# Attention: the token-row transfers of three batches placed behind later scaled x

## The chip, the cores and the metric

The kernel runs on one core of a Trainium2 chip. The metric is the device time of one execution in microseconds (us). The engines have these names in the profile: PE (TensorE, matrix products; PEld are its weight loads), DVE (VectorE), ACT (ScalarE), POOL (GpSimd) and SP (SyncE, which here issues DMAs). Each engine works through its own queue in order and waits there for semaphores that other engines or DMAs set.

## The reference, cut to what matters

Three stages follow each other: causal attention with a decay for 4 batches of 8 heads, 576 tokens and 64 channels, a mixture of 8 experts of which each token takes one, and a gated block.

```python
def _attn_ref(q, k, v, f):
    scores = scale * np.matmul(q, k.transpose(0, 1, 3, 2))
    cum = np.cumsum(np.log(np.clip(f, 0.0001, 1.0)), axis=-1)
    scores = np.where(causal, -1e9, scores + cum[:, :, :, None] - cum[:, :, None, :])
    attn = softmax(scores)                       # max, exp, sum + 1e-9
    return np.matmul(attn, v)

def _moe_ref(x, w_gate, w_output_gate, w1, w2):  # x: 2304 tokens x 512
    logits = x @ w_gate
    e_idx = np.argmax(logits, axis=1)
    ...
    for e in range(E):
        mask = e_idx == e
        ye = np.maximum(x[mask] @ w1[e], 0.0) @ w2[e]
        out[mask] = gate_w[mask, None] * eom[mask, e, None] * ye

def _moe2_ref(x, w_gate, w_val, w_out):
    return ((1 / (1 + np.exp(-(x @ w_gate)))) * (x @ w_val)) @ w_out
```

## The kernel before, in words

Attention works on pairs of heads, 16 of them, numbered `pr`; four pairs make a batch (`b, p = divmod(pr, 4)`). The 576 tokens of a pair are five tiles, four of 128 and one of 64, called the tails. A pair works on its tiles in the order (3, 2), tails, (1, 0). For each tile PE makes the scores (L472, for tails L513), DVE adds the decay, masked on POOL (L364, L374), and takes the maximum (L407), ACT takes the exponential (L412), PE transposes (L459), ACT moves the result out of PSUM (L342), and PE multiplies by v (L496, tails L534). PE then turns the product back to token rows (`turn_x`, L436), and one DVE operation for two tiles scales them by the inverse sums (`scale`, L446; the inverses are L421 and L422) and writes them into `xb[b % 2]`, the buffer of token rows of the batch: "scaled x" in the title. Tails are copied (L342 or L344). There is one PSUM buffer for the output of L436, so the next `turn_x` waits for the scale.

The order of the instructions on each engine isn't that of the code. `Flow` (from L120) collects all operations with a cost on each engine they may run on, what they read and write, and a group; a list planner places them one by one in its own time, and they are sent out sorted by the planned begin. The group (normally the pair's number) sets the urgency: a later group gives way to an earlier one.

At the end of a batch `logits` and `route` (from L573) work out the expert and the slot of each of its tokens (`sli`). Then five indirect DMAs (`scatter`, L645 to L655) write the rows of the batch, one tile each, 128 or 64 rows of 2,560 bytes, from `xb` to their slots in `x_d` in memory. POOL issues them, each followed by `unordered` (L768), which also sets a memset of the one-element tile `gap` (L772) on POOL behind each transfer. All five carry the group of the batch's last pair.

Once the rows of the first three batches have landed, SP fetches the first rows of the first expert (`ahead_rows`, L692) into a buffer, DVE weighs them (L699), and three loads of this expert's weights (`ahead_steps`, L730) follow into the same buffer, each split into two parts (L344 or L342, L736). They are `wa0` to `wa2`, which the first matmuls of the experts (L1042) read. DVE's xb buffers alternate, so a batch writes into the buffer of the batch two before it, whose transfers have to be through.

Of the kernel before, what the change touches and what calls it, by code (L numbers as in the profile page):

```python
# [17 lines left out]
B, H, S, D = 4, 8, 576, 64  # L18
NP = B * H // 2
NPB = H // 2  # L20
# [20 lines left out]
EVAC, SPLIT, LOW = ("ACT",), ("DVE", "ACT"), ("POOL", "DVE")  # L41
PERIOD, SLACK = 12000.0, 0.0
SWITCH = 95.0
NSC, NPT, NPO, NPX, NPS, NTP = 6, 3, 1, 1, 4, 2

AHEAD = ((B - 1) * S + E - 1) // E
# [73 lines left out]
class Flow:  # L120
# [39 lines left out]
    def start(self, op, e):  # L160
# [3 lines left out]
        for s in op.slots:  # L164
            if not s.taken:
# [4 lines left out]
                if len(live) + n >= s.ring.bufs:  # L170
# [3 lines left out]
                    t = max(t, self.seen(old.last, e))  # L174
        return max(t, self.free[e] + (SWITCH if e == "PE" and op.mode != self.mode else 0.0), op.after)

# [60 lines left out]
class Kern:  # L237
# [150 lines left out]
    def attn_pair(self, pr):  # L388


        nc, F, R = self.nc, self.F, self.R
        b, p = divmod(pr, NPB)
        i = pr % 2
        q, k = self.qk[pr]
        qz = self.qz[i]
        cb, cm, ct = self.decay[pr]
        vt, xb = self.vt[b], self.xb[b % 2]
# [148 lines left out]
            group_pv(ts)  # L546
        if TAILS_AT == len(GROUPS):
            tails()
        self.logits(pr)


# [19 lines left out]
    def route(self, b, pr):  # L571

        nc, F, R = self.nc, self.F, self.R  # L573
        V = nc.vector
        xb, lg = self.xb[b % 2], self.lg
        sh = [P, 5, E]
        m, m2, ls, ohb, pos, se, so, sel, px = (
            R[n].new() for n in ("m", "m2", "ls", "ohb", "pos", "se", "so", "sel", "px"))
        oh, sli = self.oh[:, b], self.sli[:, b]
        base, nbase = self.base[b], self.base[b + 1]  # L580

        def bc(a):
            return a.unsqueeze(2).to_broadcast(sh)

        def add(fn, cost, r, w):
            F.add(lambda e: fn(), cost, r=r, w=w, group=pr)

        def first():

            l = lg.t[:, :, 0:E]  # L590
            V.tensor_reduce(out=m.t, in_=l, axis=AX.X, op=ALU.max)
            V.tensor_tensor(out=oh, in0=l, in1=bc(m.t), op=ALU.is_equal)
            V.tensor_tensor(out=oh, in0=oh, in1=self.erev, op=ALU.mult)
            V.tensor_reduce(out=m2.t, in_=oh, axis=AX.X, op=ALU.max)
            V.tensor_tensor(out=ohb.t, in0=oh, in1=bc(m2.t), op=ALU.is_equal)
            V.memset(ohb.t[64:, 4], 0.0)

        def prefix():

            prf = px.t[:, 0, :6 * E]  # L600
            ohf = ohb.t.rearrange("p t e -> p (t e)")
            nc.tensor.matmul(prf[:, 0:5 * E], lhsT=self.trib, rhs=ohf, start=True, stop=False)
            for t in range(1, 5):
                nc.tensor.matmul(prf[:, t * E:5 * E], lhsT=self.oneb, rhs=ohf[:, 0:(5 - t) * E],
                                 start=False, stop=t == 4)
            for t in range(5):
                nc.tensor.matmul(prf[:, 5 * E:], lhsT=self.oneb, rhs=ohf[:, t * E:(t + 1) * E],
                                 start=t == 0, stop=t == 4)

        def place():  # L610
            pr3 = px.t[:, 0, :6 * E].rearrange("p (t e) -> p t e", e=E)
            V.tensor_tensor(out=pos.t, in0=pr3[:, 0:5], in1=base.unsqueeze(1).to_broadcast(sh), op=ALU.add)
            V.tensor_tensor(out=pos.t, in0=pos.t, in1=ohb.t, op=ALU.mult)
            with nc.allow_low_precision(reason="whole numbers below 2 ** 24"):
                V.tensor_reduce(out=sli, in_=pos.t, axis=AX.X, op=ALU.add)
            V.tensor_tensor(out=nbase, in0=pr3[:, 5], in1=base, op=ALU.add)

        def less():
            V.tensor_tensor(out=ls.t, in0=lg.t[:, :, 0:E], in1=bc(m.t), op=ALU.subtract)

        def chosen():
            V.tensor_copy(out=oh, in_=ohb.t)
            V.tensor_tensor(out=so.t, in0=ohb.t, in1=lg.t[:, :, E:], op=ALU.mult)
            V.tensor_reduce(out=sel.t, in_=so.t, axis=AX.X, op=ALU.add)

        def total():
            V.tensor_reduce(out=se.t, in_=ls.t, axis=AX.X, op=ALU.add)
            V.tensor_scalar_add(se.t, se.t, 1e-9)

        def weight():  # L630
            V.scalar_tensor_tensor(out=se.t, in0=sel.t, scalar=1.0, in1=se.t, op0=ALU.add, op1=ALU.mult)
            V.reciprocal(out=xb[:, :, 0, D], in_=se.t)

        add(first, {"DVE": 1200}, [lg], [m, ohb, m2, ("oh", b)])
        add(prefix, {"PE": 300}, [ohb, "consts"], [px])
        add(less, {"DVE": 120}, [lg, m], [ls])
        add(lambda: nc.scalar.activation(ls.t, ls.t, AF.Exp), {"ACT": 130}, [ls], [ls])
        add(chosen, {"DVE": 400}, [lg, ohb, m2], [sel, so, ("oh", b)])
        add(lambda: nc.scalar.activation(sel.t, sel.t, AF.Exp, scale=-1.0), {"ACT": 100}, [sel], [sel])
        add(place, {"DVE": 660}, [px, ohb, ("base", b), "consts"], [pos, ("base", b + 1), ("sli", b)])  # L640
        add(total, {"DVE": 300}, [ls], [se])
        mine = [("xb", b % 2, 0, t) for t in range(5)]
        add(weight, {"DVE": 300}, [se, sel], mine)

        def scatter(t):  # L645
            n = P if t < 4 else 64
            ins = nc.gpsimd.indirect_dma_start(
                out=self.x_d, out_offset=bass.IndirectOffsetOnAxis(ap=sli[:n, t:t + 1], axis=0),
                in_=xb[:n, t].rearrange("p h c -> p (h c)"), in_offset=None)
            self.unordered("scatter", ins)  # L650

        for t in range(5):
            F.add(lambda e, t=t: scatter(t), {"POOL": 1280}, move=1000, group=pr,
                  r=[("sli", b), "blank"] + [("xb", b % 2, q, t) for q in range(NPB)], w=[("rows", b, t)])
        if b == B - 2:  # L655
            self.pick(pr)

# [82 lines left out]
    def attention(self, pool):  # L740
        ac, tmp = pool("ac", 1), pool("tmp", 1)
        F = self.F = Flow(PERIOD, SLACK)
        self.vt, self.qk, self.decay = {}, {}, {}
        spec = {
            "q": ([P, S], 3), "k": ([P, S], 3), "cb": ([P, 2, S], 2), "cm": ([P, 2, 512], 2), "ct": ([P, S], 2), "sc": ([P, 512], NSC), "sct": ([P, S], 1),
            "pt": ([P, 4, 2 * P], NPT), "ptt": ([P, 4, P], 1), "vt": ([P, 4, DM], 2),
            "oT": ([P, 2 * P], 2), "sums": ([P, 9], 3), "nmx": ([P, 9], 3), "rs": ([P, 9], 3),
            "lg": ([P, 5, 2 * E], 2), "m": ([P, 5], 2), "m2": ([P, 5], 2), "ls": ([P, 5, E], 2),
            "pos": ([P, 5, E], 2), "se": ([P, 5], 2), "so": ([P, 5, E], 2), "sel": ([P, 5], 2),
        }  # L750
        self.R = {n: Ring(pool(n, k), n, s, F32, k) for n, (s, k) in spec.items()}
        self.R["ohb"] = Ring(pool("ohb", 2), "ohb", [P, 5, E], BF16, 2)
        for n, s, k in (("px", [P, 2, 2 * XW], NPX), ("ps", [P, 512], NPS), ("tp", [P, 4, P], NTP), ("po", [P, 2 * P], NPO)):
            self.R[n] = Ring(pool(n, k, space=PSUM), n, s, F32, k)
        self.attn_setup(ac, tmp)
        for e in range(E):
            F.add(lambda e_, e=e: self.blank(e), {"SP": 700}, r=["zr"], w=["blank"], group=1 + e // 4, move=2500, after=35e3 + 5e3 * e)
        for i in range(4):
            F.add(lambda e, i=i: self.clear(i), {"SP": 700}, r=["zr"], w=["clear"], group=9 + i, move=2500, after=110e3 + 12e3 * i)
        for pr in range(NP + 2):  # L760
            if pr > 1:
                self.attn_pair(pr - 2)
            if pr < NP:
                self.attn_operands(pr)
        self.ahead_steps()
        F.emit()

    def unordered(self, key, ins):  # L768

        tc = self.tc  # L770
        ins = ins.ins
        self.nc.gpsimd.memset(self.gap, 0.0)  # L772
        tc.declare_no_dep(ins, group=key, reason="each token has a row of its own")
        tc.add_to_no_dep_group(key, ins)
        self.groups.setdefault(key, []).append(ins)
# [5 lines left out]
    def behind(self, ins, w):  # L781
        self.tc.add_manual_dep(
            ins.ins, w.name, mybir.DependencyInfo(mybir.DependencyClass.Sync, mybir.DependencyReason.DATA),
            reason="comes when the other has been done")
# [925 lines left out]
```

## Time and profile before

| | us |
|---|---|
| median of 3 runs | 899.55 (898.86 to 900.95) |
| profiled execution | 899.0 |
| span of its trace | 897.3 |
| PE busy | 851.9 |
| DVE busy | 611.3 |
| ACT busy | 449.5 |
| POOL busy | 313.0 |

The trace is of one execution. Its span leaves 1.7 us outside it. PE is busy for 95% of the span; attention ends on PE at about 228 us, the experts begin at about 231 us. A row of a timeline gives the start, the duration, the engine, the line, the operation, what it writes and reads, the count (x8: eight alike, put together) and, in brackets, how long the engine had been idle before it and what ended that by the semaphores. "remote" there means that no instruction of the trace was found for it, "issue" that the profile shows nothing that was waited for. PEclk in a row of the windows is the share of TensorE's full clock that was granted: 1.00 is 2.4 GHz and 0.50 is 1.2 GHz.

### The profile page before, as it was taken

Reading aid. Unit: us, or ns where it says so; the run is one execution under the profiler, and the core shown is the slowest. Engines: PE = TensorE matmul, PEld = TensorE weight load, DVE = VectorE, ACT = ScalarE, POOL = GpSimd, SP = SyncE. Lnnn points to the kernel's source line nnn. Section 1 sums busy time; section 2 is a strip of 40 time slices with the busy share of each in tenths; the row PEclk is TensorE's granted clock in tenths of the full one; section 3 lists DMA queues with packets and bytes.
Section 4 is the critical chain, followed back from the end, with each engine's and each line's share of the span. In section 5 each row is a group of like instructions: output and inputs, shape, how many; then the busy total and the mean of one; then the engine's idle time right before and its main releaser. Section 6 shows DMA issues by size and latency. Waiting matters only on the chain. (4 is left out here: it accounts for less than half of the span.)

```text
span 897.3 us, 16056 instructions
## 1 busy us (share of the span) xinstructions
PE 851.9 (95%) x5664; PEld 752.5 (84%) x5664; DVE 611.3 (68%) x1436; ACT 449.5 (50%) x986; POOL 313.0 (35%) x383
## 2 busy tenths in 40 slices
PE   4999998989899999999998899999999999999996
PEld 2666665656799999999998799999999999999995
DVE  4767675767675677767846587989898995334544
ACT  3877776757355455546654463434343442332220
POOL 3211331131222123223225556565544466321213
PEclk9999999999899999999998999999999999999998
DMA  7799759632589667778546576777674457655631
GB/s 232 230 300 279 232 162 258 184 134 90 176 262 307 218 216 220 245 243 287 192 144 215 102 222 130 199 149 158 192 224 164 133 181 287 244 212 211 211 129 71
DMA packets 84981, 180.48 MB, mean 201 GB/s; under 512 B 10129, under 2 KB 47505, under 8 KB 83361
## 3 DMA queue, kind: packets, MB, share of 16 engines
q1 hardware_dynamic: 81345, 168.78, 61.7%
q0 software_dynamic: 3552, 10.63, 3.1%
q8 instruction: 46, 0.75, 0.3%
q14 instruction: 38, 0.31, 0.1%
HBM read 124.48 MB, written 54.90 MB: 200 GB/s over the span
## 5 line engine op out<-in xcount | busy, mean ns | idle before, releaser
L1384 PE MATMUL z<-xo,wt 128*128 128x384 f32 x432 | 87.7, 337 | 3.8 <-DVE r L1444 3.8
L1384 PE MATMUL x<-xo,wt 128*128 128x384 f32 x432 | 87.7, 337 | 2.7 <-ACT s L1395 2.0
L412 ACT ACTIVATE sc<-sc,nmx 128x512 f32<-128x512 f32 (+3 forms) x128 | 71.7, 562 | 34.9 <-DVE nmx L407 34.7
L1402 POOL TENSOR_TENSOR s<-s,s 128x384 f32<-128x384 f32 x36 | 40.2, 1116 | 139.1 <-ACT s L1401 139.1
L1384 PE MATMUL w<-xo,wt 128*128 128x384 f32 x432 | 87.6, 337 | 0.3 <-DVE r L1445 0.3
L1384 PEld LDWEIGHTS x<-xo,wt 128*128 128x128 f32 x432 | 76.7, 188 | 6.6 <-ACT s L1395 2.6
L1384 PEld LDWEIGHTS z<-xo,wt 128*128 128x128 f32 x432 | 76.8, 190 | 4.6 <-DVE r L1444 4.5
L1384 PEld LDWEIGHTS w<-xo,wt 128*128 128x128 f32 x432 | 76.7, 190 | 0.6 <-DVE r L1445 0.6
L1016 POOL TENSOR_SCALAR xg<-xr 128x512 f32<-128x512 f32 (+5 forms) x20 | 34.5, 1739 | 116.7 <-DMA xr<-x_d 116.7
L1209 POOL TENSOR_TENSOR tt<-tt 128x256 f32<-128x256 f32 x48 | 42.8, 897 | 63.2 <-DVE tt L1178 61.4
L1474 PE MATMUL po<-wo,g1h 128*128 128x512 f32 x204 | 64.3, 397 | 0.0
L1395 ACT COPY s<-x 128x384 f32<-128x384 f32 x36 | 17.3, 479 | 91.1 <-PE x L1384 83.9
L342 ACT COPY pt<-tp 128x512 f32<-128x512 f32 (+3 forms) x128 | 49.7, 424 | 21.1 <-PE tp L459 17.0
L459 PE MATMUL tp<-ident,sc 128*128 128x128 f32 x320 | 53.9, 291 | 2.3 <-ACT pt L342 1.0
L472 PE MATMUL ps<-k,q 64*128 64x512 f32 (+3 forms) x256 | 48.6, 497 | 5.7 <-DMA k<-in_kT 5.7
L459 PEld LDWEIGHTS tp<-ident,sc 128*128 128x128 f32 x320 | 36.3, 144 | 20.2 <-ACT pt L342 6.9
L1480 DVE TENSOR_TENSOR acc<-po,acc 128x512 f32<-128x512 f32 x60 | 40.0, 686 | 19.0 <-PE po L1474 18.2
L407 DVE CUSTOM_DVE_ANT_0 sc<-ps,cm 128x128 f32<-128x128 f32 x128 | 33.3, 286 | 24.5 <-PE tp L459 8.7
L364 POOL TENSOR_SCALAR_AFFINE_SELECT cm<-cb 128x512 f32<-128x512 f32 x32 | 20.4, 639 | 75.1 <-DMA cb<-cum_d 64.0
L1405 DVE TENSOR_TENSOR s<-y,s 128x384 f32<-128x384 f32 x36 | 19.9, 552 | 36.6 <-PE y L1384 36.6
L1474 PEld LDWEIGHTS po<-wo,g1h 128*128 128x128 f32 x204 | 38.2, 188 | 7.7
L407 DVE CUSTOM_DVE_ANT_0 sc<-ps,cb,nmx 128x384 f32<-128x384 f32 (+2 forms) x96 | 43.7, 479 | 0.3
(327 smaller groups left out, 2468.5 us busy)
## 6 DMA issues: line engine op xcount, KB each, us to landing
raw<-in_w SPq DMA_DIRECT2D x69, 512.0 KB
w_d<-wt SPq DMA_DIRECT2D x84, 256.0 KB
wt<-w_d SPq DMA_DIRECT2D x12, 1792.0 KB
raw<-in_wm SPq DMA_DIRECT2D x18, 1024.0 KB
cb<-cum_d SPq DMA_DIRECT2D x32, 288.0 KB
x_d<-roomf SPq DMA_DIRECT2D x8, 960.0 KB
w_d<-wo SPq DMA_DIRECT2D x24, 256.0 KB
wo<-w_d SPq DMA_DIRECT2D x6, 1024.0 KB
```

Of the source, the lines that this page charges most:

```text
L342: self.nc.scalar.copy(out, in_)
L364: F.add(lambda e, j=j: nc.gpsimd.affine_select(out=cm.t[:, j].rearrange("p (t c) -> p t c", c=P), in_=cb.t[:, j, :512].rearrange("p (t c) ...
L407: nc.vector.tensor_tensor_reduce(out=sc.t[:, cs], in0=ps.t[:, o:o + w], in1=in1(), scale=-0.125, scalar=acc if c else 3e38, op0=ALU.add, o ...
L412: F.add(lambda e: nc.scalar.activation(sc.t[:, :n], sc.t[:, :n], AF.Exp, bias=nmx.t[:, u:u + 1], scale=-1.0, accum_out=sums.t[:, u:u + 1]) ...
L459: nc.tensor.transpose(tp.t[:n, c - c0], sc.t[:, c * P:c * P + n], self.ident)
L472: nc.tensor.matmul(ps[j].t[:, :ext], lhsT=q.t[h, q0 + 64 * j:q0 + 64 * j + P], rhs=k.t[h, :ext], start=True, stop=True)
L1016: nc.gpsimd.tensor_scalar_mul(o3, x3, g)
L1209: nc.gpsimd.tensor_tensor(out=ts[:, o], in0=ts[:, a], in1=ts[:, b], op=ALU.subtract)
L1384: nc.tensor.matmul(bank, lhsT=l, rhs=r, start=first and not k and not i, stop=end and k == HK - 1 and i == 2, skip_group_check=True)
L1402: nc.gpsimd.tensor_tensor(out=s5, in0=s5, in1=s7, op=ALU.add)
L1474: nc.tensor.matmul(po, lhsT=a, rhs=b, start=i == 0, stop=i == len(mm) - 1)
L1480: nc.vector.tensor_tensor(out=acc[i], in0=po, in1=acc[i], op=ALU.add)
```

## The change

For the first three batches each of the five transfers is planned behind a scaled x of a later pair, named in a table: `SPREAD[b][t]` is (q, u), which means tile u of the pair that comes q pairs after the batch's last. The transfers of the fourth batch are left as it was. The group of a transfer is that later pair. In `unordered` the memset of `gap` becomes a copy on POOL of one element of the scaled x of that tile into `gap`. This copy stands behind the transfer on POOL, so it is the copy that waits for the scale, and what follows it on POOL's queue that is held. The number of instructions stays the same.

```diff
+SPREAD = (((2, 3), (2, 1), (3, 3), (3, 1), (4, 3)), ((1, 1), (2, 3), (2, 1), (3, 3), (3, 1)), ((1, 3), (1, 4), (1, 1), (2, 3), (2, 4)))
...
             tails()
+        for t, u, rows in self.behind_x.pop(pr, ()):
+            rows(t, pr, lambda u=u: xb[0:1, u, 2 * p, 0:1], [("xb", b % 2, p, u)])
         self.logits(pr)
...
-        def scatter(t):
+        def scatter(t, behind):
             n = P if t < 4 else 64
             ins = nc.gpsimd.indirect_dma_start(
                 out=self.x_d, out_offset=bass.IndirectOffsetOnAxis(ap=sli[:n, t:t + 1], axis=0),
                 in_=xb[:n, t].rearrange("p h c -> p (h c)"), in_offset=None)
-            self.unordered("scatter", ins)
-
-        for t in range(5):
-            F.add(lambda e, t=t: scatter(t), {"POOL": 1280}, move=1000, group=pr,
-                  r=[("sli", b), "blank"] + [("xb", b % 2, q, t) for q in range(NPB)], w=[("rows", b, t)])
+            self.unordered("scatter", ins, behind)
+
+        def rows(t, pr, behind=None, r=()):
+            F.add(lambda e: scatter(t, behind and behind()), {"POOL": 1280}, move=1000, group=pr,
+                  r=[("sli", b), "blank", *r] + [("xb", b % 2, q, t) for q in range(NPB)], w=[("rows", b, t)])
+
+        if b == B - 1:
+            for t in range(5):
+                rows(t, pr)
+        else:
+            for t, (q, u) in enumerate(SPREAD[b]):
+                self.behind_x.setdefault(pr + q, []).append((t, u, rows))
...
-    def unordered(self, key, ins):
+    def unordered(self, key, ins, behind=None):
...
-        self.nc.gpsimd.memset(self.gap, 0.0)
+        if behind is None:
+            self.nc.gpsimd.memset(self.gap, 0.0)
+        else:
+            self.nc.gpsimd.tensor_copy(out=self.gap, in_=behind)
```

## Rows read from the trace of the kernel before

**Rows 1.** Windows: stretch, its us; each engine's busy us (count); PEclk; DMA share; GB/s.

```profile
72.96:86.37 13.41, 13.04 (x125) 8.76 (x123) 10.85 (x63) 10.10 (x34) 1.75 (x4) 1.00 0.92 292
86.37:100.18 13.81, 11.66 (x107) 8.02 (x107) 7.47 (x45) 9.89 (x32) 6.82 (x13) 1.00 0.95 313
100.18:112.01 11.83, 11.80 (x109) 8.02 (x108) 8.63 (x44) 9.29 (x31) 1.98 (x5) 1.00 0.47 136
124.92:142.92 18.00, 13.58 (x116) 8.62 (x116) 10.83 (x64) 9.27 (x31) 6.73 (x13) 0.91 0.79 228
179.37:196.48 17.11, 12.68 (x112) 8.30 (x111) 10.70 (x68) 9.24 (x31) 6.32 (x13) 0.90 0.42 145
240.00:892.00 652.00, 641.85 (x3851) 607.32 (x3850) 451.04 (x612) 288.72 (x470) 253.26 (x248) 0.99 0.64 200
```

**Rows 2.** PE waits, 80:205: what for; total us, times, longest.

```profile
PE px L436 <- DVE xb L446: 8.2, 2, 4.2
PE px L436 <- DVE rs L421: 1.6, 1, 1.6
```

**Rows 3.** Timeline of POOL, transfers: start, us, engine, line, what, [idle before, releaser].

```profile
92.75 0.91 POOL L647 DMA_INDIRECT x_d<-xb,sli  x1 [0.23 <-issue]
...
129.64 0.98 POOL L647 DMA_INDIRECT x_d<-xb,sli  x1 [0.93 <-DVE nmx L407]
...
132.19 0.96 POOL L647 DMA_INDIRECT x_d<-xb,sli  x1 [0.21 <-issue]
...
134.72 0.90 POOL L647 DMA_INDIRECT x_d<-xb,sli  x1 [0.22 <-issue]
...
186.56 0.96 POOL L647 DMA_INDIRECT x_d<-xb,sli  x1 [0.21 <-issue]
...
189.10 0.90 POOL L647 DMA_INDIRECT x_d<-xb,sli  x1 [0.22 <-issue]
```

**Rows 4.** Timelines of DVE, PE and ACT beside the three bursts.

```profile
94.65 0.49 DVE L446 TENSOR_TENSOR xb<-px,rs 128x320 f32<-128x320 f32 x1 [3.48 <-PE tp L459]
...
132.29 1.09 PE L459 MATMUL tp<-ident,sc 128*128 128x128 f32 x8
...
136.80 0.49 DVE L446 TENSOR_TENSOR xb<-px,rs 128x320 f32<-128x320 f32 x1 [3.52 <-remote]
...
136.86 1.07 ACT L342 COPY pt<-tp 128x512 f32<-128x512 f32 x2 [2.99 <-remote]
...
186.82 0.59 ACT L342 COPY pt<-tp 128x512 f32<-128x512 f32 x1 [1.03 <-PE px L436]
...
191.37 0.49 DVE L446 TENSOR_TENSOR xb<-px,rs 128x320 f32<-128x320 f32 x1 [4.12 <-remote]
```

**Rows 5.** Windows behind the second and third burst, columns as in rows 1.

```profile
137.80:141.21 3.41, 3.41 (x10) 1.32 (x10) 0.92 (x7) 1.01 (x5) 0.00 (x0) 0.50 1.01 358
192.41:195.83 3.42, 3.42 (x12) 2.06 (x14) 1.94 (x14) 2.42 (x9) 0.24 (x1) 0.50 0.42 145
```

**Rows 6.** Timeline of DVE: two scales (L446) of the third batch's transfers.

```profile
185.00 0.47 DVE L446 TENSOR_TENSOR xb<-px,rs 128x320 f32<-128x320 f32 x1
...
201.31 0.48 DVE L446 TENSOR_TENSOR xb<-px,rs 128x320 f32<-128x320 f32 x1
```

**Rows 7.** Timelines of SP, DVE and PE towards the first expert.

```profile
195.08 0.97 SPq L692 DMA_DIRECT2D roomf<-x_d  x2
...
205.16 0.48 DVE L699 TENSOR_SCALAR roomf<-roomf 128x512 f32<-128x512 f32 x1
...
206.55 14.28 SPq L730 DMA_DIRECT2D roomf<-in_w  x3
...
210.03 0.76 DVE L344 CAST wa0h<-roomf 128x512 fp32r<-128x512 f32 x2 [0.52 <-DMA roomf<-in_w]
...
224.24 0.75 DVE L344 CAST wa2h<-roomf 128x512 fp32r<-128x512 f32 x2
...
237.93 0.27 PE L1042 MATMUL ph<-xah,wa2h 128*128 128x216 f32 x1
```

More of the change, by code (lines that the diff above doesn't have):

```diff
@@ L742, in attention @@
         F = self.F = Flow(PERIOD, SLACK)
-        self.vt, self.qk, self.decay = {}, {}, {}
+        self.vt, self.qk, self.decay, self.behind_x = {}, {}, {}, {}
         spec = {
```

## The prediction

> **What bounds the kernel now.** I read the busy time of TensorE (PE) by stretches first. From 240 us to 892 us, the experts and the gated block after them, it is busy for 641.85 of 652 us at a clock of 0.99 [rows 1]. Nothing the change touches can shorten that stretch, so a microsecond won or lost in attention should arrive at the end whole. Next I cut attention into one stretch for each pair of heads, from one pair's second group of value products to the next pair's, and looked for stretches in which PE isn't busy for nearly all of the time [rows 1]. An undisturbed pair takes 11.83 us, 11.80 of them busy. The pair in which the first batch is routed (logits, slots) takes 13.41, and still 13.04 are busy: the route alone stops nobody. Three stretches stand out: 13.81 us with 11.66 busy, 18.00 with 13.58 and 17.11 with 12.68. The clock is 1.00 in the first and 0.91 and 0.90 in the others.
>
> Then I asked the waits what PE waited for in there: 8.2 us, in two pieces, for the scale that writes x (L446, a VectorE operation), and 1.6 for the inverse ahead of one (L421) [rows 2]. In the timelines these fall together with the five token-row transfers that POOL issues in a row: each takes 0.90 to 0.98 us and the next starts some 1.27 after it [rows 3]. What the reader is to see there: VectorE's scale starts at 94.65, 136.80 and 191.37 after 3.48, 3.52 and 4.12 us of idleness, and in the second burst ScalarE comes back in the same instant, at 136.86 after 2.99 [rows 4]. Those moments are 0.99 us (94.65 less 92.75 + 0.91), 1.18 and 1.37 after the end of the last transfer of each burst [rows 3, 4]. Yet PE had long done its part: in the second burst its transposes ran from 132.29 and were through at 133.38 [rows 4], and their reader started 3.5 us later. So results of PE are there, and the engines that wait for PE don't go on until the burst is over. Work that followed the first transfer of the second burst, at 129.64, and the second, 1.27 behind it, still went through; what ended under the third, from 132.19, did not. In the third burst ScalarE was let go at 186.82, after 1.03 us, under the third transfer (186.56) [rows 3, 4]. My reading: three or more of these transfers close together hold back the news of PE's work; one or two do not, or barely. No row says by what means.
>
> After the second and third burst PE, having stood for about 4 us, runs at a granted clock of 0.50 for 3.41 and 3.42 us (1.2 instead of 2.4 GHz) [rows 5].
>
> **The change part by part.** *Removed:* the three bursts. Two sums for what they cost. By waits and clock: 8.2 + 1.6 = 9.8 us of waiting [rows 2], and half of 3.41 + 3.42 us at half clock, 3.4 [rows 5]: 13.2. By stretches [rows 1]: 13.81 − 11.83 = 2.0, then 18.00 − 13.41 = 4.6 and 17.11 − 13.41 = 3.7, since the last two hold a route as well: 10.3. The second takes the route's own extra work out and leaves in what PE catches up afterwards, the first takes the waits whole. I take the middle, 11.7, and keep 10.3 and 13.2 as ends. A clean pair as the yardstick for all three would give even 2.0 + 6.2 + 5.3 = 13.5.
>
> *Added:* no transfer; the same 15 go out one by one. A transfer t+1 comes behind a copy that waits for a named scale, and for the first two batches these are five different scales of three or four pairs; a pair lasts 11.83 us and has two, so the transfers come some 6 us apart on average [rows 1]. For those I charge nothing, because the first two of a burst held nobody up; the price if that fails is in the rivals. The third batch is packed tighter: transfers 0 and 1 are let go by the scale at 185.00, while transfers 2 and 3 stand behind the tails and the second scale of the same pair, at about 188 to 189 once the 4 us of hold are gone, and transfer 4 behind the scale at 201.31 [rows 3, 6]. That is two packs of two. A pack of two I charge with nothing to 1.03 us, the dearest wait beside the beginning of a burst [rows 4]; two packs, I take 1.0 in all, with 0 and 2.1 as the ends.
>
> *Fifteen copies for fifteen memsets.* On POOL, which a pair's stretch keeps busy for 1.8 to 6.8 of 12 to 18 us [rows 1]. The trace has no one-element copy; between nothing and the 0.47 us of a whole scale on VectorE [rows 6] the fifteen cost POOL at most 7 us, spread over ten pairs. What matters is what is queued behind the wait: the next transfer, and the masks of the following pairs (affine selects, L364 and L374), whose output VectorE needs. In the second burst, which holds the queue for 6 us, the masks stood behind all of it, and yet VectorE stopped at a scale, which needs no mask [rows 4]. Cost: nothing, as long as the masks run ahead of their pair; if a copy is late by more than that lead, VectorE waits for the difference. I leave up to 1 us in the range for this.
>
> *Moved:* the last rows of the third batch. SyncE's fetch of these rows stands at 195.08, the weighing on VectorE at 205.16, the split of the last of three weights at 224.24, and the first matmul that needs it at 237.93 [rows 7]. With the change the last transfer comes behind the scale at 201.31 instead of at 189.10 [rows 3, 6]. Copy (0.3), the transfer (1.0) and a landing of about 3 us put the fetch at 205.6; the fetch itself I set at 3.5, from the weight load of 206.55 whose split starts at 210.03 [rows 7]. The weighing is then possible at 209.1 instead of 205.16, 4 us late, and the last weight 4 us later, at about 230 where 237.93 needs it. So 7 us of slack are left and I charge nothing. If that cover is gone, PE waits at its first expert.
>
> *Sum:* 11.7 − 1.0 = 10.7 us. The profiled execution took 899.0 us, 897.3 of span and 1.7 around it, so 888.3 on its basis. The median of the runs, 899.55, lies 0.55 above the profiled one; on that basis 888.85, and I say **888.8 us**.
>
> **A rule that speaks against this.** The rows show PE's finished work unseen by VectorE and ScalarE for 3 us and more beside a burst [rows 4]. The Trainium skill, SBUF — State Buffer, "Who interferes with whom", says that only the port pair shared by VectorE and GpSimd makes engines wait, that a DMA never contends with a compute engine, and that PE and ACT never wait on anyone. By that rule the transfers could not be the cause, and separating them would save nothing: it is the first rival below. The trace speaks against it, since ScalarE stands as long as VectorE does, 2.99 beside 3.52 us.
>
> **The rivals.** *1. No change.* The stall is not due to the transfers' closeness, or the transfers stay close. The second could be: the copy stands behind its transfer, so transfer 0 isn't gated by its own scale at all, and if POOL comes late to its queue, all waits are already met and the five run back to back as now. For it: only the order on POOL's queue separates them. Against it: POOL has time to spare [rows 1], and the first stall comes not in the routed pair (13.04 of 13.41 busy) but in the pair with the burst. Time: 899.5.
>
> *2. The third batch keeps its stall.* Two packs of two with some 3 us between them may act as one burst, as the data of the first pack are still under way. Then 4.2 + 1.7 us of the 13.2 stay [rows 2, 5], and the gain is 5 to 6: 894.
>
> *3. The chain to the first expert is late.* If the landing or the three weight loads slip by over 7 us, or VectorE's queue, which is in order, stands before the last scale for a weight that isn't there, PE waits; a slip of 10 costs 3: 892.
>
> *4. Slower.* Every lone transfer holds PE's news for about as long as the third of a burst did at first: 1.03 us [rows 4]. Now nothing is saved by letting five holds overlap: 15 × 1.03 = 15.5 us of holds against 11.7 saved, 903, the more so if a hold lands on the narrow ring of PSUM buffers each time. It decides from 11.7 / 15 = 0.78 us per transfer. Against it: beside the first transfers of the bursts no such wait appears in VectorE's rows. A smaller hold, 0.3, would take 4.5 of the gain.
>
> **How the numbers follow.** Forecast, a gain of 7 to 14 (10.3 to 13.5, less holds of 0 to 3 us of the lone transfers, packs and masks): 0.64, 885.5 to 892.5. Rival 2: 0.13, 892.5 to 895.5. Rival 3: 0.05, about 892. Rival 1: 0.08. Rival 4: 0.10, above 901. To hold 8 in 10 the range takes in the forecast, rival 3 and most of rival 2: 885 to 895. A measurement of this kernel can tell about 0.2% (1.8 us) from no change. Faster by more than that: 0.64 + 0.13 + 0.05 = 0.82. Same: 0.08. Slower: 0.10.
>
> **What would show it.** Right: POOL's 15 transfers of the first three batches stand 3 us and more apart, but for two pairs in the third; the idleness of 3.5 to 4.1 us ahead of L446 is gone; the stretches of 18.00 and 17.11 shrink to 13 to 14; no clock of 0.50 behind them; PE's waits for L446 and L421 under 2 us in all. Wrong: five short waits on PE results per batch (rival 4), a hold in the pair behind the third route (rival 2), PE idle ahead of the first expert's matmuls (rival 3), or transfers that still follow at 1.27 us (rival 1). What would upset all of it is a hold that goes by the bytes in flight rather than by how many transfers follow closely: then other traffic beside a lone one would do the same.

## The result and the profile after

The changed kernel takes 887.5 us (median of 6 runs, 885.95 to 891.69) beside 899.69 for the kernel before (6 runs), a ratio of 0.9864 (0.9849 to 0.9879). The profiled execution of it took 887.1 us, with a span of 885.4, 11.9 under the one before. One thing has to be said at once, because the experiments can't be read without it: in three of the five sets of runs made for this study the kernel before, unchanged, took about 885 us, and not 899. In the one of these three in which the changed kernel was run as it is, it took 0.7% longer and saved nothing. The two kinds of sets are kept apart below.

The stretches of the changed kernel are cut at the same places as [rows 1]: the pair that had the first burst, the pair that is routed for the second batch, the two pairs behind the third route, then the end of attention up to the experts' first matmul, and 652 us of the experts.

```profile
86.41:97.95 11.54, 11.53 (x108) 8.00 (x107) 7.86 (x45) 9.76 (x32) 2.59 (x4) 1.00 0.99 251
...
122.69:135.15 12.46, 11.79 (x116) 8.05 (x115) 10.46 (x64) 9.04 (x31) 2.89 (x5) 1.00 0.71 180
171.71:182.38 10.67, 10.48 (x108) 7.20 (x109) 9.93 (x63) 8.43 (x28) 3.81 (x6) 1.00 0.25 88
182.38:195.68 13.30, 12.94 (x117) 8.89 (x114) 8.57 (x49) 10.81 (x36) 4.25 (x10) 1.00 0.35 113
195.68:219.67 23.99, 18.19 (x188) 13.10 (x187) 16.50 (x62) 14.01 (x45) 3.76 (x3) 1.00 0.25 72
228.00:880.00 652.00, 642.09 (x3859) 608.76 (x3858) 451.05 (x612) 289.11 (x471) 254.01 (x249) 0.99 0.64 201
```

The same end of attention and the two pairs behind the third route in the kernel before, for the comparison:

```profile
208.35:231.15 22.80, 18.75 (x193) 13.34 (x191) 16.14 (x65) 13.53 (x44) 3.90 (x3) 0.97 0.39 135
179.37:208.35 28.98, 24.45 (x218) 16.49 (x217) 19.79 (x114) 18.62 (x62) 7.59 (x15) 0.94 0.33 107
```

The first burst's pair went from 13.81 to 11.54 us (2.3 saved), the second's from 18.00 to 12.46 (5.5), the two pairs behind the third route from 28.98 to 10.67 + 13.30 = 23.97 (5.0). That is 12.8. The end of attention gave 1.2 of it back (23.99 beside 22.80). The other stretches make up the rest to 11.9. The clock is 1.00 in all of attention's stretches shown here. The stretch in the experts is as full of work as before.

PE's waits from 80 to 200 us in the changed kernel (what for; total us, times, longest) answer to [rows 2]: 0.5 us for the scale, now L447, where 8.2 stood, and none for the inverse, now L422.

```profile
PE px L437 <- DVE xb L447: 0.5, 2, 0.2
```

POOL's timeline shows the transfers of the third batch, the most tightly packed (start, us, engine, line, what, idle before). The first three start 2.9 and 2.3 us apart, then a pack of two follows 1.37 apart; [rows 3] had five of them 1.27 apart. A copy takes 0.18 us, one of the fifteen 0.40.

```profile
176.34 1.00 POOL L650 DMA_INDIRECT x_d<-xb,sli  x1 [3.03 <-DVE nmx L408]
178.89 0.18 POOL L785 COPY gap<-xb 1x1 f32<-1x1 f32 x1 [1.56 <-DVE xb L447]
179.22 0.98 POOL L650 DMA_INDIRECT x_d<-xb,sli  x1 [0.16 <-issue]
...
181.53 0.98 POOL L650 DMA_INDIRECT x_d<-xb,sli  x1 [0.51 <-issue]
...
190.10 1.02 POOL L650 DMA_INDIRECT x_d<-xb,sli  x1 [0.16 <-issue]
...
191.47 0.92 POOL L650 DMA_INDIRECT x_d<-xb,sli  x1 [0.16 <-issue]
```

Where the 1.2 us at the end went is seen in three timelines of the changed kernel, VectorE, POOL and PE ahead of the last route:

```profile
214.96 0.43 DVE L345 CAST wa1h<-roomf 128x512 fp32r<-128x512 f32 x1 [3.23 <-DMA roomf<-in_w]
215.31 0.48 DVE L447 TENSOR_TENSOR xb<-px,rs 128x320 f32<-128x320 f32 x1
215.89 2.15 DVE L570 TENSOR_TENSOR lg<-lg,xb 128x80 f32<-128x80 f32 x2
...
215.47 2.48 POOL L746 TENSOR_TENSOR wa1l<-roomf,wa1h 128x512 fp32r<-128x512 f32 x2 [4.72 <-DVE wa1h L345]
...
219.40 0.19 PE L605 MATMUL px<-ohb,trib 128*128 128x40 bf16 x1 [4.50 <-DVE ohb L599]
```

and in the kernel before:

```profile
228.99 0.52 DVE L567 TENSOR_TENSOR lg<-lg,xb 128x80 f32<-128x80 f32 x2
...
230.85 0.21 PE L602 MATMUL px<-ohb,trib 128*128 128x40 bf16 x1 [2.51 <-DVE ohb L596]
```

PE waits 4.50 us for the route's first result instead of 2.51, 2.0 us more. VectorE's last scale stands behind the split of the second weight, which waits 3.23 us for its data; of that only 0.4 us count, since PE's product for this scale was done at 214.89 (before the change the scale started 0.05 us after it). The other 1.6 us are the two additions to the logits behind it, which take 2.15 us instead of 0.52, beside two subtractions on POOL that ran from 215.47 to 217.95. The Trainium skill, SBUF — State Buffer, "Who interferes with whom", has that a VectorE operation with two inputs in SBUF contends with a GpSimd operation that reads SBUF; these operations are of that kind, and the 2.15 beside 0.52 agrees.

### The profile page after: what moved, and what is told of

It is laid out like the page before. It is cut to its first block, busy times and chain, and to the rows that moved or that the text cites. A ratio compares the mean times of both kernels' runs of the same rounds, so it can differ in the third digit from the quotient of the medians.

```text
span 885.4 us, 16052 instructions
## 1 busy us (share of the span) xinstructions
PE 847.3 (96%) x5664; PEld 750.6 (85%) x5664; DVE 612.6 (69%) x1433; ACT 450.8 (51%) x989; POOL 314.9 (36%) x383
## 5 line engine op out<-in xcount | busy, mean ns | idle before, releaser
L1397 PE MATMUL y<-xo,wt 128*128 128x384 f32 x216 | 43.2, 334 | 0.0
```

Of the source, the lines that this page charges most:

```text
L1397: nc.tensor.matmul(bank, lhsT=l, rhs=r, start=first and not k and not i, stop=end and k == HK - 1 and i == 2, skip_group_check=True)
```

## The experiments

The theory on trial is that of the prediction: transfers close together hold back the news of PE's work (*packing*). The rival: the gain comes from where the transfers stand and from the order that the planner finds around them (*place and order*).

### All five behind one later scale (packed_late)

```diff
-SPREAD = (((2, 3), (2, 1), (3, 3), (3, 1), (4, 3)), ((1, 1), (2, 3), (2, 1), (3, 3), (3, 1)), ((1, 3), (1, 4), (1, 1), (2, 3), (2, 4)))
+SPREAD = (((2, 3),) * 5, ((2, 3),) * 5, ((1, 3),) * 5)
```

> All five transfers of a batch stand behind one scaled x of a later pair (first two batches: the first scale two pairs after the route; third: the first scale of the pair after it), so they are away from the route as after the change, but close together as before it. Theory of packing (three or more transfers some 1.3 us apart hold the news of PE's work until 1.0 to 1.4 us after the last): VectorE and ScalarE stand for 3 to 4 us beside each burst again, 9 to 10 us of PE waits and perhaps the half clock behind them come back, and the time is 896 to 900 us. Theory of place and order (the gain comes from where the transfers stand and from the order that the planner finds around them): no hold, 887 to 889 us.

It took 895.41 us beside 899.36 for the kernel before, a ratio of 0.9960 (0.9943 to 0.9977). Two long holds came back at the new places, as the rows of VectorE, ScalarE and POOL show:

```profile
96.22 0.49 DVE L447 TENSOR_TENSOR xb<-px,rs 128x320 f32<-128x320 f32 x1 [2.80 <-PE tp L460]
...
152.95 0.29 DVE L408 CUSTOM_DVE_ANT_0 sc<-ps,cm 128x128 f32<-128x128 f32 x1 [2.51 <-remote]
...
98.05 0.21 ACT L343 COPY oT<-po 128x64 f32<-128x64 f32 x1 [2.56 <-remote]
...
96.07 0.93 POOL L650 DMA_INDIRECT x_d<-xb,sli  x1 [0.16 <-issue]
...
152.24 0.92 POOL L650 DMA_INDIRECT x_d<-xb,sli  x1 [0.16 <-issue]
```

Its windows have the burst's pair at 17.15 us and a clock of 0.87 in the first batch, and 15.11 us in the pair behind the second batch's burst:

```profile
85.18:102.33 17.15, 13.97 (x107) 8.69 (x106) 8.44 (x47) 9.97 (x32) 7.61 (x13) 0.87 0.90 287
...
151.49:166.60 15.11, 12.86 (x110) 8.27 (x108) 9.43 (x50) 9.81 (x32) 4.14 (x10) 1.00 0.90 302
178.60:192.90 14.30, 13.40 (x119) 8.77 (x117) 10.99 (x64) 9.80 (x32) 6.88 (x13) 1.00 0.44 151
```

Neither theory has it whole. Packed again, the kernel loses about 8 of the 12 us, although the transfers are off the route: packing is the larger part. But some 4 stay won, because a hold costs only what is waiting for PE just then; beside the third burst, packed as before but for its first transfer, the pair is at 14.30, near the 13.30 to 13.41 of a pair with a route. There VectorE and ScalarE went on at 191.31 and 191.36, 1.0 us after the last transfer, but had stood for only 1.05 and 0.95 us. The end of a hold isn't always 1.0 us behind the burst: ScalarE's at 98.05 is, but the two waits of VectorE above end while the last transfer is still being issued. The time is just under the 896 to 900 us of the first theory.

### The kernel before, with its transfers 2.5 us apart (burst_spaced)

```diff
         self.nc.gpsimd.memset(self.gap, 0.0)
+        if len(self.groups.get(key, ())) < 15:
+            for _ in range(2):
+                self.nc.gpsimd.memset(self.pad, 0.0)
```

> The kernel before, in its own order, with two memsets of 64 by 640 elements on POOL (0.72 us each in the trace of before) behind each transfer of the first three batches, so that these start some 2.7 us apart instead of 1.27. Theory of packing: the holds are gone or shrink to under 0.5 us each, and 8 to 12 us are gained, 888 to 892 us; up to 3 us less if the masks queued behind the longer burst come late. Theory of place and order: the same order, so 898 to 901 us.

It took 906.58 us, 1.0086 (1.0063 to 1.0108) of the kernel before. The total says nothing on the question: the condition lets memsets into two later uses of `unordered` as well, 60 beside the 30 that were meant, in the experts and the last stage. Attention, with the 30, can be read. Its windows and PE's longest wait there:

```profile
84.65:96.40 11.75, 11.59 (x107) 8.00 (x106) 8.20 (x40) 9.88 (x32) 8.57 (x15) 1.00 0.95 305
96.40:114.83 18.43, 14.23 (x109) 9.63 (x108) 9.24 (x46) 9.61 (x31) 6.50 (x14) 0.81 0.47 143
127.73:141.03 13.30, 12.01 (x117) 8.28 (x116) 11.71 (x64) 9.05 (x31) 9.06 (x15) 1.00 0.68 175
177.46:189.75 12.29, 11.34 (x111) 7.64 (x111) 11.55 (x64) 8.50 (x28) 7.69 (x14) 1.00 0.34 112
...
102.14 1.30 PE L514 MATMUL ps<-k,qz 128*128 128x288 f32 x2 [3.56 <-DVE nmx L408]
...
100.58 0.29 DVE L408 CUSTOM_DVE_ANT_0 sc<-ps,cm 128x128 f32<-128x128 f32 x1 [4.34 <-POOL cm L365]
```

With the order of the kernel before and the transfers at the same places, only further apart, the pairs with bursts are at 11.75, 13.30 and 12.29 us instead of 13.81, 18.00 and 17.11 [rows 1], at full clock. That speaks for packing and against place and order. The price of a longer burst is the mask: those of the next pair stand behind it on POOL, VectorE waited 4.34 us for one and PE 3.56 for VectorE, with a low clock behind it (18.43 us, 0.81). Attention as a whole ended 6.6 us earlier (first expert's matmul at 224.52 instead of 231.15). The change avoids this price, because masks are planned between its transfers.

### Packs of 2, 3 and 4 (packs)

```diff
-SPREAD = (((2, 3), (2, 1), (3, 3), (3, 1), (4, 3)), ((1, 1), (2, 3), (2, 1), (3, 3), (3, 1)), ((1, 3), (1, 4), (1, 1), (2, 3), (2, 4)))
+SPREAD = (((2, 3), (2, 3), (3, 3), (3, 3), (3, 3)), ((2, 3), (2, 3), (2, 3), (2, 3), (3, 3)), ((1, 3), (1, 4), (1, 1), (2, 3), (2, 4)))
```

> The changed kernel with packs of other sizes: first batch 2 and 3, second batch 4 and 1, third as in the change. Theory of packing with a count: no hold beside the 2, a hold of 1 to 2 us beside the 3, of 2 to 3 us beside the 4, each over about 1 us after the pack's last transfer; 889 to 892 us. Theory of place and order: no hold at any, 887 to 889 us. If a hold goes by any two transfers close together, the pack of 2 shows one of 0.5 us or more too.

One execution: 891.75 us. The pairs with the pack of 2, the pack of 3 and the pack of 4, and the pair behind that; then POOL's last transfer of the four and the start of VectorE behind it:

```profile
85.03:96.57 11.54, 11.53 (x108) 8.00 (x107) 7.71 (x45) 9.77 (x32) 3.97 (x7) 1.00 0.97 298
96.57:109.65 13.08, 12.36 (x112) 8.22 (x111) 9.06 (x46) 9.39 (x31) 5.65 (x11) 1.00 0.67 211
133.33:145.39 12.06, 11.85 (x108) 8.17 (x107) 7.67 (x42) 9.78 (x35) 5.58 (x10) 1.00 1.00 269
145.39:161.23 15.84, 13.85 (x109) 8.78 (x108) 9.77 (x50) 9.82 (x32) 3.54 (x9) 1.00 0.88 290
...
144.81 0.98 POOL L650 DMA_INDIRECT x_d<-xb,sli  x1 [0.16 <-issue]
...
146.80 0.29 DVE L408 CUSTOM_DVE_ANT_0 sc<-ps,cm 128x128 f32<-128x128 f32 x1 [2.46 <-remote]
```

Two together cost nothing. Beside three there is no wait of 1.6 us or more on VectorE or ScalarE; the pair is 1.2 us over a clean one. Beside four VectorE stood for 2.46 us, until 1.01 us after the last was issued (144.81 + 0.98). That is the order that packing with a count expects, with one execution for each size; but a hold of 1 to 2 us beside three was expected, and there the longest wait for PE on ScalarE is 1.05 us.

### Plain bursts from SyncE and from POOL (plain_bursts)

```diff
+        if pr in (6, 10):
+            old = self.xb[1 - b % 2]
+            for t in range(5):
+                def more(e, t=t):
+                    n = P if t < 4 else 64
+                    eng = nc.sync if pr == 6 else nc.gpsimd
+                    eng.dma_start(out=self.s_d[pr // 10, t, :n], in_=old[:n, t].rearrange("p h c -> p (h c)"))
+                F.add(more, {"SP" if pr == 6 else "POOL": 1280}, r=[("xb", 1 - b % 2, q, t) for q in range(NPB)] + [("xb", b % 2, p, 3)], w=["more"], group=pr)
```

> The changed kernel with two bursts added: five plain transfers of the same 128 or 64 rows of 2560 bytes from the other buffer to a scratch in memory, in pair 6 from SyncE's queue and in pair 10 from POOL's. If a hold goes by the bytes or by the number of transfers in flight, PE's readers stand for 2 to 4 us in both pairs; if it goes by POOL making the descriptors, only in pair 10; if only by indirect transfers, in neither. SyncE's are issued some 0.4 us apart, so bytes would show there first.

One execution: 889.24 us. SyncE's five went out from 105.90 within 3.86 us, some 0.8 us apart and not 0.4, with an indirect one of POOL just before them, and the pair is as long as a clean one (first row below). POOL's are seen in its timeline: six transfers start within 5 us, from 156.30 to 161.12, two of them indirect ones of the second batch (three of the plain ones are left out here; the fifth followed only at 169.56), and that pair is 11.62 us long (last row).

```profile
100.30:112.13 11.83, 11.80 (x109) 8.04 (x107) 8.63 (x44) 9.29 (x31) 5.51 (x11) 1.00 0.82 267
...
157.21 1.02 POOL L658 DMA_INDIRECT x_d<-xb,sli  x1 [0.30 <-issue]
...
159.24 0.95 POOL L658 DMA_INDIRECT x_d<-xb,sli  x1 [0.30 <-ACT sc L413]
...
161.12 0.57 POOL L558 DMA_DIRECT2D s_d<-xb  x1
...
149.54:161.16 11.62, 11.59 (x108) 7.84 (x104) 8.77 (x42) 9.39 (x31) 6.75 (x13) 1.00 0.94 251
```

Neither a burst of as many bytes from SyncE nor POOL's issuing of four plain transfers makes a hold by itself. What is left is the indirect transfers, more than two or three of them close together. This kernel had no such group in attention, so it shows what doesn't hold, not what does.

### The same bursts, and no hold (quarter_rows, quarter_columns, burst_pad1, before_again)

The next set of runs, on the same chip as the four above, had the kernel before at 884.80 us (23 runs, 883.23 to 886.34). Two kernels in it were to tell bytes from rows, a third to space the bursts less:

quarter_rows:

```diff
-            n = P if t < 4 else 64
+            n = 32 if t < 4 else 16
```

quarter_columns:

```diff
-                out=self.x_d, out_offset=bass.IndirectOffsetOnAxis(ap=sli[:n, t:t + 1], axis=0),
-                in_=xb[:n, t].rearrange("p h c -> p (h c)"), in_offset=None)
+                out=self.x_d.rearrange("r (a c) -> (r a) c", a=4), out_offset=bass.IndirectOffsetOnAxis(ap=sli[:n, t:t + 1], axis=0),
+                in_=xb[:n, t, :2].rearrange("p h c -> p (h c)"), in_offset=None)
```

burst_pad1 (pad is a tile of 64 by 640):

```diff
         self.nc.gpsimd.memset(self.gap, 0.0)
+        if key == "scatter" and len(self.groups.get(key, ())) < 15:
+            self.nc.gpsimd.memset(self.pad, 0.0)
```

> The kernel before with its bursts, but each transfer moves only the first 32 (16 of the last tile) of its 128 (64) rows, so later stages compute with rows that are missing; bytes and rows both a quarter. If the hold goes by what a transfer moves, by bytes or by rows, the waits of 3.5 to 4.1 us ahead of the scale beside the first three bursts go to under 1 us and the time is 887 to 891 us. If it goes by the number of indirect transfers alone, the waits stay at 3 us and more, unless each transfer takes POOL so much less time that the burst itself is shorter: then hold and burst shrink alike.

> The kernel before with its bursts, but each row of a transfer is cut to its first 640 of 2560 bytes (rows go to other places of the same array, so later stages compute with other data); as many rows, a quarter of the bytes. If the hold goes by bytes: no hold, 887 to 891 us, as with a quarter of the rows. If it goes by rows (one address worked out for each) or by the number of transfers: waits of 3 us and more as before, 897 to 901 us.

> The kernel before in its own order, with one memset of 64 by 640 elements on POOL behind each transfer of the first three batches only, so they start some 1.95 us apart. With two memsets, 2.5 us apart, the waits ahead of the scale were gone in attention, at the price of 3.6 us for a late mask (that kernel had the memsets in a later stage too, which made its total long). Theory of packing: most of the hold goes, waits of under 1.5 us per burst, and the burst is 2.7 us longer, so a mask may cost 0 to 2 us: 889 to 895 us. Theory of place and order: 898 to 901 us. If the hold is only stretched with the burst, each wait grows by 2 us: 903 to 907 us.

They took 882.07 and 885.45 us (one execution each) and 887.99, a ratio of 1.0036 (1.0021 to 1.0051). With no hold in the kernel before beside them, the first two tell nothing of its cause. burst_pad1 fits none of its expectations; it is a little slower. VectorE waited 0.8 us in it for late masks; what the rest of the 3 us went to isn't shown.

So the kernel before was run again with a trace:

> The kernel before once more, unchanged, for a trace from the same session on the chip as its neighbours. In one session the kernel before took 899.4 us (10 runs), in the next 884.8 (23 runs), with nothing changed. Theory that the hold of PE's news is there in some sessions and not in others: either 898 to 901 us with the three waits of 1.6, 4.0 and 4.2 us ahead of the scale and the half clock, or 883 to 887 us with none of them, and nothing in between. Theory that something else differs between sessions (transfers, clock): 884 to 886 us with the waits still there.

It took 885.53 us beside 885.16 for itself. The first theory's second branch is what came. Its second burst on POOL, the scale beside it, and the three stretches with bursts:

```profile
127.15 0.98 POOL L647 DMA_INDIRECT x_d<-xb,sli  x1 [1.23 <-DVE nmx L407]
...
129.70 0.96 POOL L647 DMA_INDIRECT x_d<-xb,sli  x1 [0.22 <-issue]
...
130.72 0.49 DVE L446 TENSOR_TENSOR xb<-px,rs 128x320 f32<-128x320 f32 x1
...
86.18:97.71 11.53, 11.52 (x108) 8.00 (x107) 7.39 (x45) 9.76 (x32) 6.59 (x12) 1.00 0.93 298
122.45:135.20 12.75, 11.88 (x116) 7.89 (x115) 10.74 (x64) 9.09 (x31) 6.67 (x13) 1.00 0.67 177
171.64:182.99 11.35, 11.05 (x112) 7.39 (x111) 10.61 (x68) 8.40 (x28) 6.15 (x12) 1.00 0.38 130
```

The burst is the same: transfers 1.27 us apart, 0.96 each [rows 3]. The scale that started at 136.80 after 3.52 us of idleness [rows 4] starts with no wait, in the middle of the burst. The pairs are as short as after the change: 11.53 beside 11.54, 12.75 beside 12.46, and 23.58 beside 23.97 for the two behind the third route.

One more mark tells the two kinds of sets apart. The page's part on DMA issues gives the time to landing in the sets without the hold, and for no group of transfers in those with it, the kernel before and the changed one alike. The first row is of the kernel before in the result's runs, the second of before_again:

```profile
cb<-cum_d SPq DMA_DIRECT2D x32, 288.0 KB
...
cb<-cum_d SPq DMA_DIRECT2D x32, 288.0 KB, 6.0
```

Landings are worked out from the events of the transfers' semaphores, so traces with the hold seem to lack some of those; the trace of before holds 10,531 events of semaphores, that of before_again 11,057. Whether that has the same cause as the hold, or whether taking the trace has a part in the hold, is open.

### The changed kernel where there is no hold (after_again)

The kernel is the changed one, as it is.

> The changed kernel once more. Theory that the change takes out only the hold: 886 to 889 us in any session, so a ratio of 0.985 to 0.988 where the kernel before takes 899, and of 1.001 to 1.004 where it takes 885, since the late chain to the first expert costs its 2 us ahead of the routing either way. Theory that sessions shift both kernels alike: 0.985 to 0.988 in any.

It took 889.84 us (4 runs, 887.30 to 893.12) beside 885.16, a ratio of 1.0070 (1.0047 to 1.0092): the first theory's direction, and more than its size. In the profiled executions the experts' first matmul came at 219.57 instead of 217.97 us, since PE waited 4.41 us for the last route instead of 2.51; the spans differ by 2.5 us, the medians by 4.7. The profiled execution was the fastest of the four, so what the others lost beyond that isn't shown. The clock adds a scatter of its own: over the first 13.90 us of the experts PEclk was 0.77 here and 0.88 in before_again, but 0.88 in the first trace of the changed kernel, with a wait of 4.50 us, and 0.78 in the next kernel, chain_earlier, with one of 2.51. So it didn't go by the length of that wait.

### The third batch's rows earlier (chain_earlier, chain_earlier_2)

```diff
-SPREAD = (((2, 3), (2, 1), (3, 3), (3, 1), (4, 3)), ((1, 1), (2, 3), (2, 1), (3, 3), (3, 1)), ((1, 3), (1, 4), (1, 1), (2, 3), (2, 4)))
+SPREAD = (((2, 3), (2, 1), (3, 3), (3, 1), (4, 3)), ((1, 1), (2, 3), (2, 1), (3, 3), (3, 1)), ((1, 3), (1, 1), (1, 4), (2, 3), (2, 3)))
```

> The changed kernel, with the third batch's transfers placed behind (1,3), (1,1), (1,4), (2,3), (2,3): the last is no longer planned behind the tails two pairs later but with the fourth. Theory that the wait of 4.5 us ahead of the last routing (2.5 before the change) comes from the late chain of fetch, weighing and weight splits on VectorE and POOL: the wait falls to 2.5 to 3.5 us, and 0.5 to 2 us are gained, 885.5 to 887 us. Theory that nothing hangs on it, or that the new order costs elsewhere: 887 to 889 us.

> The changed kernel with the third batch's transfers behind (1,3), (1,1), (1,4), (2,3), (2,3) once more. Where the kernel before takes 899 us beside it, the ratio is 0.983 to 0.987, 1 to 2 us better than the change's own 0.986, since the wait ahead of the last routing is 2.5 instead of 4.5 us; where it takes 885, the ratio is 1.001 to 1.004 again, and the change itself gave 1.007. If the wait ahead of the last routing is not what costs, it is 0.985 to 0.988 or 1.005 to 1.009.

Both ran without the hold. The first took 886.47 us beside 884.80, 1.0022 (1.0008 to 1.0035), the second 884.52 beside 884.69, 1.0000 (0.9988 to 1.0012), just under the 1.001 to 1.004 that was expected, where the change itself, in another set, was at 1.0070. In the trace of the second, PE's last wait is what it was before the change (the additions ahead of it stand in the first row):

```profile
215.98 0.52 DVE L570 TENSOR_TENSOR lg<-lg,xb 128x80 f32<-128x80 f32 x2
...
217.84 0.19 PE L605 MATMUL px<-ohb,trib 128*128 128x40 bf16 x1 [2.50 <-DVE ohb L599]
```

So the late chain to the first expert is what made PE's last wait longer, and this table takes that back: 2.50 us instead of 4.41, with the additions at 0.52 again and no subtraction on POOL beside them. The table moves more than the fifth transfer, since the second and third scales change places too; the fifth starts at 190.46 instead of 192.11. The experts' first matmul comes at 218.11 instead of 219.57, 1.5 us earlier; the rest of the 4.7 us between the medians isn't accounted for. This version has the same spread for the first two batches, so it should keep their part of the gain where the hold is; it wasn't run there.

### Bytes or rows once more (mixed_quarters)

```diff
+            if b == 1:
+                n //= 4
+            dst, src = self.x_d, xb[:n, t]
+            if b == 0:
+                dst, src = dst.rearrange("r (a c) -> (r a) c", a=4), xb[:n, t, :2]
```

> The kernel before with its bursts, but the first batch's rows cut to a quarter of their bytes (as many rows), the second batch's to a quarter of the rows, and the third batch's left whole as the control, so later stages compute with rows that are missing or in other places. Only where the hold shows at all on the chip (the kernel before at 898 to 901 us beside it, and 3 us or more ahead of the scale at the third burst) does it tell anything on the first two: a hold by bytes leaves neither of them (waits under 1 us), a hold by rows leaves it at the first alone, a hold by the number of indirect transfers leaves it at both. Where the kernel before takes 885 us, all three show under 0.5 us, and the time is 883 to 886 us.

It took 883.21 us beside 884.69, 0.9982 (0.9970 to 0.9994), and the control, the third batch's full burst, had no hold. As the expectation says, that leaves bytes, rows and number undecided.

## Why the prediction was right, and where it was not

**The time.** 888.8 was forecast, 887.5 was measured, within 885 to 895, and by the mechanism that was forecast as far as that goes: the waits beside the bursts and the half clock behind them are gone. That it came within 1.3 us is in part luck, since the errors below cancel: 1.1 us more was removed than the sum had, the packs cost nothing where 1.0 was charged, and the end of attention, charged with nothing, took 1.2. It is luck too that the runs of the result were of the kind with the hold. The prediction knew of no other, and where there is no hold the gain that it forecast isn't there.

**Removed.** The sum had 11.7, between 10.3 by stretches and 13.2 by waits. The stretches of after against before give 12.8, near the upper end: a pair with a route, the yardstick of 13.41, was too long for the later batches. The second's came out at 12.46, and the two pairs behind the third route together at 23.97, where 13.41 + 11.83 = 25.24 was reckoned.

**Packs of the third batch.** Charged with 1.0 us, they cost nothing that can be seen; transfers 0 and 1 were 2.9 us apart, not close, and a pack of 2 cost nothing in the kernel with packs.

**Copies and masks.** A copy is 0.18 us, 0.40 at most, inside the bounds of 0 and 0.47. No mask was late in the changed kernel. That the masks were a real risk is shown by the burst with memsets, where one cost PE 3.56 us.

**The chain to the first expert.** This step failed. It charged nothing because the last weight would be there 7 us before PE needs it. That cover held: the last weight's split started at 221.49 and its first matmul at 226.81. But the chain was mis-sized and the wrong consumer looked at. Against the experts' first matmul the weighing came 10 us later and not 4 (15.6 us ahead of it instead of 26.0), so that the second weight's splits fell on the end of attention. There one stands in VectorE's queue ahead of the last scale (0.4 us), and POOL's subtractions run beside the last additions (1.6 us); PE's wait for the route grew by these 2.0 us. Rival 3 named the queue ahead of the last scale, which is the smaller part; the sum and the rivals had nothing for VectorE and POOL in each other's way.

**Slower by lone transfers, and no change.** Rival 4 did not come: no waits beside lone transfers. Rival 1 said that the stall might not be due to closeness. Where the hold exists, the kernels with bursts moved, spaced and in smaller packs are against it. But the sentence that three or more transfers close together hold back the news of PE's work was told as if it held always. The same burst at the same spacing held nothing in three sets of runs, on three chips, one of which had shown the hold in another set. And the trace of before itself, which has the hold, has a burst without one: the fourth batch's five transfers, beside the first expert. They start from 232.98 on, the last four 1.3 us apart. POOL's fifth, the last matmul that ScalarE's next operation reads, and this operation:

```profile
239.03 0.90 POOL L647 DMA_INDIRECT x_d<-xb,sli  x1 [0.22 <-issue]
...
239.16 0.27 PE L1042 MATMUL ph<-xah,wa2l 128*128 128x216 f32 x1
...
239.46 0.35 ACT L1048 ACTIVATE ha0h<-ph 128x216 fp32r<-128x216 f32 x1 [2.49 <-issue]
```

ScalarE went on 0.03 us after that matmul's end, under the fifth transfer, where each of the first three bursts kept VectorE until 1.0 to 1.4 us behind its last one [rows 3, 4]. Closeness is then needed for the hold, as far as these runs show, and not enough, not even in an execution that has holds. What else is needed is open, and so is whether the hold goes by bytes, rows or number of indirect transfers. All the runs from which the trace of before came had the hold, and nothing in that trace could have told that others would not; its burst without a hold could have been seen.

**The rule of the Trainium skill** that PE and ACT never wait on anyone (SBUF — State Buffer, "Who interferes with whom") stands there among rules on the ports of SBUF. The 2.99 us for which ScalarE stood beside the second burst were idleness ahead of an operation that reads PE's output [rows 4], not a slower access of SBUF. So the traces with the hold don't speak against the rule, and the prediction asked more of it than it says when it took it to rule out any effect of the transfers.

## What to carry to other kernels

A stall of two engines at once that wait for work which a third has visibly finished points at what runs beside it; spread that out, and put real work between its pieces, not idling, because whatever is queued behind a longer stretch comes later. When a step is moved, follow it to every queue that its late result passes through, not only to the last consumer. And measure an unchanged kernel in several sets of runs before a stall is put down to its code: here a gain of 1.4% in one kind of set is a loss of 0.7% in the other.

## What was not expected of the hardware

The kernel before takes 899 us in some sets of runs and 885 in others, with nothing between (896.1 to 901.6 and 883.2 to 886.4), on one and the same chip too; of the 14.2 us between the two spans, 897.3 and 883.1, 2.3 lie in the first burst's pair, 5.2 in the second's and 5.4 in the two pairs from the third route on. And where the hold exists, two readers of PE were let go together: at the end of the second burst VectorE went on at 136.80 and ScalarE at 136.86 [rows 4], with results of PE that were finished about 1 us apart; at the end of the first burst it was 94.65 and 94.75. Had PE itself been stopped, its results should have come that far apart again, so it looks as if the news was kept and not the work. This is argued from a few rows and not shown, and not every hold ended so: with the bursts moved, VectorE went on at 96.22 and ScalarE at 98.05.
